# The gated recurrence of a fused kernel, its steps written in another order: transposes between the score halves, counts last, three score banks

## The chip, the cores and the metric

The kernel runs on one core of one Trainium2 chip. The time is the device time of one execution in microseconds, the median of several runs. The profile is of one further execution, and its times are microseconds from the start of its span. PE is the tensor engine, DVE the vector engine, ACT the scalar engine, POOL the GpSimd engine and SP the engine that issues most of the loads.

## The reference

Two blocks follow one another. The first is a gated linear recurrence over the sequence, for each of 4 batches and 8 heads with 768 positions and 48 channels. The second sends each of the 3072 rows to one of 8 experts.

```python
f = 1.0 / (1.0 + np.exp(-f_logit))                       # (4, 8, 768, 48)
for t in range(S):
    state = f[:, :, t, :, None] * state + np.einsum('bhd,bhe->bhde', k[:, :, t], v[:, :, t])
    y[:, :, t] = np.einsum('bhd,bhde->bhe', q[:, :, t], state)

x = y.transpose(0, 2, 1, 3).reshape(3072, 384)
logits = x @ w_gate                                       # (3072, 8)
expert_idx = np.argmax(logits, axis=1)
gate_w = softmax(logits)[np.arange(N), expert_idx]        # with 1e-9 in the denominator
for e in range(8):                                        # rows sorted by expert
    y_sorted[lo:hi] = np.maximum(x_sorted[lo:hi] @ w1[e], 0.0) @ w2[e]   # 384 -> 1024 -> 384
out = gate_w[:, None] * y_sorted[inv_perm]
```

## The kernel before

**The units.** The sequence is cut into 6 chunks of 128 positions, and the batches into two pairs, which gives 12 units (`NU = 12`). A unit holds two batches with 8 heads each; two heads lie above one another on the 128 partitions, so that a tile has 8 segments (`SEG`) of 128 positions, 1024 columns. Each unit has tiles `q`, `k`, `v` and `f`, all float32, of half a megabyte each. Units u and u + 2 follow one another in the sequence: the state of one is the input of the other.

**What is done to a unit.** The functions, with their lines:

- `growth` (L361, L362): ACT takes exp(-f), and POOL adds one, which gives 1/f.
- `product` (L369): a DVE scan multiplies these up along the positions into the tile `r`. There is one `r` for all units, so the scan of a unit waits until everybody has read the `r` of the unit before.
- `by_r` (L381, L382): POOL multiplies `k` by `r`, and copies the last column.
- `log_r` (L386) and `decay` (L392, L395): ACT takes the logarithm of `r` and the exponential of its negative, with a load of its function table before each; POOL copies the last column.
- `by_decay` (L400): DVE multiplies `q` by it.
- `score` (L412, L415): PE multiplies k and q into score tiles `s`, and DVE copies them with the causal mask into `at`. Here a score tile takes two banks of the accumulator, and there are two such tiles (the pool `pss`).
- `keys` (L427, L428): PE transposes `k` into two tiles `kp`, and ACT copies them into `kn`.
- `within` (L436) and `before` (L457): PE sums the output `yt` from the scores and v, and from the old state and q.
- `added` (L473) and `update` (L488, L490, L491): PE multiplies `kn` and v into `dp`, DVE adds the old state, and POOL multiplies the sum by the last decay.
- `settle` (L498): ACT copies `yt` into `ys`.
- `rows` (L518, L528, L533, L535): PE turns `ys` into rows with gate logits (`xp`), ACT copies the rows into `xr`, and DVE sums the logits into `lg`.

The small tiles `kp`, `xp`, `dp`, `rp` and `etp` share the pool `pst` under one tag, with two banks before.

**The routing.** For every second unit (and for each of the last two) `rows` returns a `Route` with methods that are called through the step: `choose` (DVE, L189 to L197) finds the expert of each row, `count` (PE, L201, L202) sums the chosen ones into `rp`, `place` (DVE, L208 to L226) turns the sums into positions, `weigh` (ACT, L229) and `fill` (DVE, L233 to L235) give the weights, and `send` (POOL, L164) scatters the rows into a buffer in memory.

**The order.** The loop over `n` runs 14 steps, from 0 to 13. Step n takes the scores of unit n, the outputs of unit n - 1 and the rows of unit n - 2, and it prepares units n + 1 and n + 2. The whole stretch stands under `manual_schedule` with all five engines: each engine runs its instructions in the order in which the code is written, and the planner adds only the waits. So a step's order is that of the calls in the loop, for each engine by itself.

Before the loop the first unit is prepared in halves (`ab`). The constants come in by four kinds of loads on ACT's queue: a mask (`mpack`), a table of 537.5 KB (`fpack`) with the identity and much else, and four pieces of the gate's weights that are written into `fpack`. These loads are written outside the written order, so the planner places them.

**The experts.** From step 12 on the first two expert tiles run between the last steps (`widen`, `narrow`; L266 and L280), and then 22 tiles of 128 rows, each with 48 matmuls of L266 and 16 of L280. The change does not touch these.

Of the kernel before, what the change touches and what calls it, by code (L numbers as in the profile page):

```python
# [19 lines left out]
C = 128  # L20
# [92 lines left out]
def kernel(  # L113
# [21 lines left out]
    nc.scalar.dma_start(mpack, nc.inline_tensor(mv, name="c_mpack").ap())  # L135
    nc.scalar.dma_start(fpack, nc.inline_tensor(fv, name="c_fpack").ap())
# [15 lines left out]
    halves = [(a, slice(DP * a, DP * a + D)) for a in range(2)]  # L152

    for a, r in halves:
        for b, cols in enumerate((slice(XW, WX), slice(0, E))):
            nc.scalar.dma_start(
                wx[r, :, cols],
                moe_w_gate.rearrange("(p two d) e -> two d p e", two=2, d=D)[a ^ b],
            )
# [167 lines left out]
    with ExitStack() as st:  # L327
        ld = st.enter_context(tc.tile_pool(name="ld", bufs=4))
        wk = st.enter_context(tc.tile_pool(name="wk", bufs=2))
        pss = st.enter_context(tc.tile_pool(name="pss", bufs=2, space=PSUM))  # L330
        psy = st.enter_context(tc.tile_pool(name="psy", bufs=1, space=PSUM))
        pst = st.enter_context(tc.tile_pool(name="pst", bufs=2, space=PSUM))
# [72 lines left out]
        def score(u):  # L405
            x = units[u]
            x["at"] = scores[u % 2]
            for a in range(2):
                ps = pss.tile([128, 2, HP, C], F32, name="s")
                for p, h, r in heads():  # L410
                    s = HP * a + p
                    nc.tensor.matmul(  # L412
                        ps[:, h, p], lhsT=x["k"][r, s], rhs=x["q"][r, s], start=True, stop=True
                    )
                nc.vector.copy_predicated(  # L415
                    x["at"][:, a].rearrange("p h s c -> p (h s) c"),
                    _bc(causal, 1, SEG),
                    ps.rearrange("p h s c -> p (h s) c"),
                )

        def keys(u):
            x = units[u]
            x["kn"] = wk.tile([128, SEG, C], F32, name="kn", bufs=1)
            for a in range(2):
                kp = pst.tile([128, HP, C], F32, name="kp", **tr)
                for p in range(HP):
                    nc.tensor.transpose(kp[:, p], x["k"][:, HP * a + p], ident)  # L427
                nc.scalar.copy(x["kn"][:, HP * a : HP * a + HP], kp)  # L428
# [120 lines left out]
        load(2, "fkqv")  # L549
        for part in ab:  # L550
            growth(0, part)
        for part in ab:
# [4 lines left out]
        for t in scores:  # L557
            nc.vector.memset(t, 0.0)
# [4 lines left out]
        product(1)  # L563

# [440 lines left out]
```

## Time and profile before

| what | value |
|---|---|
| median of 3 runs | 457.75 us (456.74 to 458.6) |
| the profiled execution | 455.68 us |
| its span in the profile | 453.8 us |
| PE busy | 409.9 us (90%) |
| DVE, ACT, POOL busy | 160.6, 124.0, 115.6 us |
| granted clock of PE, mean | 0.963 |
| first score matmul (unit 0) | 16.3 us |
| first score matmul of unit 11 | 136.5 us |
| first expert matmul of L280 | 161.2 us |

The page of a profile gives busy times by engine, the same in 40 slices, the chain of work that ended last, and groups of instructions by line. The trace behind it answers further questions: the timeline shows each instruction with its start, its length and, in square brackets, the idle time of its engine before it with the one that ended it; a view by stretches gives the busy time of each engine between chosen moments, with the granted clock of PE (1.00 is full speed). PEld is the loading of weights into PE, which overlaps its matmuls. A float32 matmul is two instructions in the trace, a transpose one.

### The profile page before, as it was taken

The numbers are of one execution on the slowest core, as the hardware profiler recorded it, in microseconds if no ns is written. First come the engines' busy times: TensorE is split into PE (matmuls) and PEld (weight loads), VectorE is DVE, ScalarE is ACT, GpSimd is POOL, SyncE is SP. The second block draws the span as 40 slices with busy tenths as digits, with TensorE's granted clock in tenths as the row PEclk, the third lists the DMA queues.
The fourth block names the chain that finished last, engine by engine and source line by source line (L and its number), as shares of the span: only waits on it lengthen the run. The fifth ranks groups of instructions, "written<-read, shape, count | busy, mean of one in ns | idle before, by whom it ended". The sixth has DMA issues, their size and how long they took to land.

```text
span 453.8 us, 8502 instructions
## 1 busy us (share of the span) xinstructions
PE 409.9 (90%) x3580; PEld 330.1 (73%) x3581; DVE 160.6 (35%) x325; ACT 124.0 (27%) x184; POOL 115.6 (25%) x133
## 2 busy tenths in 40 slices
PE   0478898989898998999999999999999999999992
PEld 0478787878797885888888888847688887777460
DVE  3866969494964452111111111122111122111110
ACT  3689787676764300000000000001000000000010
POOL 3654466666653420001100000000100000000000
PEclk9969998888979998999999999999999999999998
DMA  8999985597922233989991550730189999000000
GB/s 288 402 381 390 378 311 187 216 382 310 361 78 85 81 113 94 402 318 358 387 361 39 189 181 19 236 114 1 42 300 396 393 390 374 28 17 19 17 2 21
DMA packets 42861, 98.32 MB, mean 217 GB/s; under 512 B 3856, under 2 KB 27717, under 8 KB 42816
## 3 DMA queue, kind: packets, MB, share of 16 engines
q1 hardware_dynamic: 38496, 87.48, 52.9%
q0 software_dynamic: 3200, 9.64, 5.6%
q10 hardware_dynamic: 1120, 0.59, 0.4%
q8 instruction: 29, 0.48, 0.4%
q14 instruction: 16, 0.13, 0.1%
HBM read 81.46 MB, written 16.63 MB: 216 GB/s over the span
## 4 chain that ended last, share of the span: by engine, by line
PE 81%; ACT 10%; DVE 3%; issue 2%; POOL 1%; DMA 1%; POOLq 0%; ACTq 0%
PE hps L266 26%; PE yps L280 25%; PE s L412 6%; PE xp L518 5%; PE dp L473 3%; ACT L392 3%; PE yp L280 3%; ACT f L392 2%; PE s L266 2%; PE hps L785 2%; PE yps L813 2%; ACT f L361 2%; PE etp L253 2%; PE yt L457 2%; ACT xr L528 1%
## 5 line engine op out<-in xcount | busy, mean ns | idle before, releaser
L266 PEld LDWEIGHTS hps<-xT,w1t 128*128 128x128 f32 x1056 | 121.1, 192 | 7.3 <-issue 2.3
L266 PE MATMUL hps<-xT,w1t 128*128 128x128 f32 x1056 | 121.8, 275 | 0.0
L280 PE MATMUL yps<-w2t,hT 128*128 128x384 f32 x352 | 117.2, 486 | 0.0
L280 PEld LDWEIGHTS yps<-w2t,hT 128*128 128x128 f32 x352 | 65.2, 190 | 40.8
L164 POOL DMA_INDIRECT out_dram<-ysb,dst x26 | 25.3, 971 | 257.3 <-DVE ysb L287 257.3
L274 ACT ACTIVATE hT<-hps 128x512 f32<-128x512 f32 x22 | 13.1, 597 | 222.6 <-PE hps L266 222.6
L276 DVE TENSOR_SCALAR hT<-hps 128x512 f32<-128x512 f32 x22 | 15.2, 692 | 106.2 <-PE hps L266 101.1
L412 PE MATMUL s<-q,k 64*128 64x128 f32 x384 | 33.2, 340 | 16.7 <-POOL last L395 16.3
L287 DVE TENSOR_SCALAR ysb<-yps,xrow 128x384 f32<-128x384 f32 x22 | 13.6, 618 | 92.9 <-PE yps L280 92.9
L412 PEld LDWEIGHTS s<-q,k 64*128 64x128 f32 x384 | 30.6, 246 | 17.3 <-POOL last L395 16.0
L369 DVE TENSOR_TENSOR_SCAN r<-f,cap 128x1032 f32<-128x1032 f32 (+1 forms) x13 | 28.7, 2208 | 13.6 <-POOL f L362 13.6
L415 DVE COPY_PREDICATED at<-mpack,s 128x1024 f32<-128x1024 uint8 x24 | 30.6, 1312 | 6.1 <-PE s L412 6.1
L164 POOL DMA_INDIRECT xs<-xr,posi x24 | 26.4, 1098 | 21.6 <-DVE xr L235 6.8
L381 POOL TENSOR_TENSOR k<-k,r 128x1024 f32<-128x1024 f32 (+1 forms) x13 | 26.4, 2030 | 2.5 <-DVE r L369 2.4
L518 PE MATMUL xp<-fpack,ys 128*128 128x104 f32 x192 | 24.3, 280 | 0.8 <-ACT ys L498 0.8
L518 PEld LDWEIGHTS xp<-fpack,ys 128*128 128x128 f32 x192 | 22.4, 192 | 2.4 <-ACT ys L498 1.0
L436 PE MATMUL yt<-at,v 128*64 128x128 f32 x384 | 23.7, 277 | 0.0
L436 PEld LDWEIGHTS yt<-at,v 128*64 128x64 f32 x384 | 20.8, 138 | 1.3 <-issue 0.2
L473 PE MATMUL dp<-v,kn 128*64 128x48 f32 x320 | 14.7, 259 | 6.8 <-ACT kn L428 6.8
L473 PEld LDWEIGHTS dp<-v,kn 128*64 128x64 f32 x320 | 13.3, 172 | 9.6 <-ACT kn L428 8.3
L400 DVE TENSOR_TENSOR q<-q,f 128x1024 f32<-128x1024 f32 (+1 forms) x13 | 14.7, 1136 | 14.0 <-ACT f L392 14.0
L427 PE MATMUL kp<-fpack,k 128*128 128x128 f32 x96 | 14.4, 285 | 4.7 <-ACT kn L428 2.8
(108 smaller groups left out, 361.3 us busy)
## 6 DMA issues: line engine op xcount, KB each, us to landing
qw<-in_moe_w_dram SPq DMA_DIRECT2D x16, 1536.0 KB, 12.3
w1t<-in_moe_w_dram SPq DMA_DIRECT2D x8, 1536.0 KB, 8.8
w2t<-in_moe_w_dram SPq DMA_DIRECT2D x8, 1536.0 KB, 13.1
xs<-pad SPq DMA_DIRECT2D x8, 800.0 KB, 12.9
v<-in_vu_dram SPq DMA_DIRECT2D x12, 512.0 KB, 6.4
f<-in_fu_dram SPq DMA_DIRECT2D x11, 516.0 KB, 8.2
k<-in_ku_dram SPq DMA_DIRECT2D x11, 512.0 KB, 9.0
q<-in_qu_dram SPq DMA_DIRECT2D x11, 512.0 KB, 6.5
```

Source lines behind the costliest of these rows:

```text
L164: ins = nc.gpsimd.indirect_dma_start(out=dst, out_offset=bass.IndirectOffsetOnAxis(ap=idx, axis=0), in_=src, in_offset=None, bounds_check= ...
L266: nc.tensor.matmul(hp[g][:, f, :], lhsT=w[0][:, j, b * 128 : b * 128 + 128], rhs=x["xT"][:, j, :], start=j == 0, stop=j == KD - 1,)
L276: nc.vector.tensor_scalar(x["hT"][:, 4:8], hp[1], 0.0, None, op0=OP.max)
L280: nc.tensor.matmul(yp, lhsT=x["hT"][:, f, :], rhs=w[1][:, f, :], start=f == 0, stop=f == NF - 1)
L369: nc.vector.tensor_tensor_scan(x["r"][:, part].rearrange("p s c -> p (s c)"), x["f"][:, part].rearrange("p s c -> p (s c)"), cap[:, part]. ...
L381: nc.gpsimd.tensor_tensor(k, k, r[:, :, 1:CR], op=OP.mult)
L392: nc.scalar.activation(dec, dec, AF.Exp, scale=-1.0)
L412: nc.tensor.matmul(ps[:, h, p], lhsT=x["k"][r, s], rhs=x["q"][r, s], start=True, stop=True)
L415: nc.vector.copy_predicated(x["at"][:, a].rearrange("p h s c -> p (h s) c"), _bc(causal, 1, SEG), ps.rearrange("p h s c -> p (h s) c"),)
L436: nc.tensor.matmul(x["yt"][DP * (h ^ a) : DP * (h ^ a) + DP, a, p], lhsT=x["v"][:, a, 2 * p + h], rhs=x["at"][:, a, h, p], start=p == 0, s ...
L473: nc.tensor.matmul(x["dp"][r, s], lhsT=x["kn"][:, s, r], rhs=x["v"][:, a, 2 * p + h, 0:D], start=s == 0, stop=True, skip_group_check=True,)
L518: nc.tensor.matmul(xp[:, p], lhsT=x["ys"][:, a, p], rhs=wx[:, p, 0:XW] if a else wx[:, p, E:WX], start=True, stop=True,)
```

## The change

The steps of the loop get another order, with some pools and loads:

- The scores of a unit are taken in two halves, and the transposes `keys` with their copies (now a function of its own, `keep`) stand between them. Each half has two tiles of one bank, and DVE copies each by itself. The pool of score tiles has three banks, the pool `pst` three.
- `product` of unit n + 2 moves from late in the step to behind the scores; `decay` comes before `within`; `before` follows `within` directly.
- `by_decay` is done in halves, and comes after `before`, ahead of `added` and `update`.
- `count`, `place` and `fill` come last in a step, after `update`.
- `growth` runs for unit n + 3 in place of n + 2, and f is loaded one unit further ahead, apart from k, q and v.
- Ahead of the loop the two `scores` tiles are zeroed before the first exponential, one on DVE and one on POOL, and the constants are loaded after the two halves of the first `growth`, in the written order.

The core of the diff:

```diff
-    nc.scalar.dma_start(mpack, ...)
-    nc.scalar.dma_start(fpack, ...)
...
+    def load_consts():
+        nc.scalar.dma_start(mpack, nc.inline_tensor(mv, name="c_mpack").ap())
+        nc.scalar.dma_start(fpack, nc.inline_tensor(fv, name="c_fpack").ap())
+        for a, r in halves:
+            for b, cols in enumerate((slice(XW, WX), slice(0, E))):
+                nc.scalar.dma_start(wx[r, :, cols], moe_w_gate...[a ^ b])
...
-        pss = st.enter_context(tc.tile_pool(name="pss", bufs=2, space=PSUM))
+        pss = st.enter_context(tc.tile_pool(name="pss", bufs=3, space=PSUM))
-        pst = st.enter_context(tc.tile_pool(name="pst", bufs=2, space=PSUM))
+        pst = st.enter_context(tc.tile_pool(name="pst", bufs=3, space=PSUM))
...
-        def score(u):
+        def score(u, a):
...
+            ps = [pss.tile([128, HP, C], F32, name="s") for h in range(2)]
+            for p, h, r in heads():
+                s = HP * a + p
+                nc.tensor.matmul(
+                    ps[h][:, p], lhsT=x["k"][r, s], rhs=x["q"][r, s], start=True, stop=True
                 )
+            for h in range(2):
+                nc.vector.copy_predicated(x["at"][:, a, h], _bc(causal, 1, HP), ps[h])
...
+        def keep(u):
+            for a in range(2):
+                nc.scalar.copy(units[u]["kn"][:, HP * a : HP * a + HP], units[u]["kp"][a])
...
         load(2, "fkqv")
+        load(3, "f")
+        nc.gpsimd.memset(scores[1], 0.0)
+        nc.vector.memset(scores[0], 0.0)
         for part in ab:
             growth(0, part)
+        load_consts()
...
-        for t in scores:
-            nc.vector.memset(t, 0.0)
...
         growth(1)
         product(1)
+        growth(2)
```

The loop's step before and after, without the expert pieces of steps 12 and 13 (the sends of a count are queued after `fill` in both):

```python
# before
score(n); settle(n-2); by_r(n+1); log_r(n+1); one send
rows(n-2); choose; within(n-1); count
decay(n+1); growth(n+2); weigh; by_decay(n+1)
keys(n); place; fill; product(n+2)
before(n-1); added(n); update(n); load(n+3, "fkqv")

# after
settle(n-2); score(n, 0); by_r(n+1); log_r(n+1); one send
keys(n); keep(n); score(n, 1); product(n+2)
rows(n-2); choose; decay(n+1); growth(n+3); weigh
within(n-1); before(n-1); by_decay(n+1) in halves
added(n); update(n); count; place; fill
load(n+4, "f"); load(n+3, "kqv")
```

## The prediction

> **What bounds the kernel now.** I read the page first, for the shares and for section 2, then busy time by stretch, with the stretches cut at the first score matmul (L412) of each step, then the chain of work, then the timeline of VectorE (DVE) and GpSimd (POOL).
>
> The stretches. Columns: stretch, length, busy time of PE, PEld, DVE, ACT and POOL with instruction counts, granted clock, DMA share, GB/s.
>
> ```profile
> 35.00:56.40 21.40, 17.82 (x286) 16.04 (x282) 16.86 (x30) 17.91 (x26) 10.87 (x12) 1.00 1.02 386
> 78.60:102.60 24.00, 21.95 (x312) 19.71 (x310) 17.31 (x30) 17.52 (x26) 14.81 (x16) 0.86 0.82 304
> 102.60:126.50 23.90, 21.84 (x310) 19.63 (x310) 17.11 (x33) 17.42 (x26) 14.80 (x16) 0.86 0.87 327
> 72.09:75.50 3.41, 2.08 (x25) 1.70 (x29) 2.92 (x9) 2.66 (x5) 3.10 (x4) 0.98 0.19 73
> 75.50:78.91 3.41, 3.41 (x61) 2.96 (x54) 3.31 (x6) 2.32 (x4) 0.72 (x1) 0.50 0.50 159
> ```
>
> The steps start at 16.3, 27.0, 35.2, 44.7, 56.4, 65.9, 78.6, 89.8, 102.6, 113.8, 126.5 and 136.5 us (n = 0 to 11); the first expert matmul of L280 starts at 161.2. A pair of steps took 21 us early and 24 us later. The difference is the clock: it stands at 0.50 for 6.7 us in each late pair (75.4 to 82.2, 99.3 to 106.1, 123.2 to 130.0), and each time it fell after 3.4 us in which PE was busy 2.1. From 180 us to the last tiles PE is hardly ever without work, and nothing there is changed, so the change moves only the moment at which the experts begin.
>
> The chain through one pair. Columns: start, length, work.
>
> ```profile
> 63.35 0.95 ACT f L361
> 64.31 0.48 ACT kn L428
> 64.83 1.16 PE dp L473 x32
> 65.99 1.99 PE s L412 x32
> 67.98 1.99 PE xp L518 x16
> 69.98 0.54 ACT xr L528 x2
> 70.55 1.28 ACT L392
> 71.84 1.06 ACT f L392
> ...
> 75.15 1.65 PE yt L457 x32
> 76.80 1.88 PE dp L473 x32
> ```
>
> A step is a ring over PE and ACT: `dp` waits for the copies `kn`, these stand on ACT behind two exponentials, these behind `xr`, which waits for `xp`, and `xp` for the scores. Its sum is 9.5 us, against 9.0 us of PE work at full clock (s 1.98, xp 1.98, yt 1.9, kp 1.03, the part on the old state 1.02, dp 1.07); a count adds 0.43. The last two lines run at half clock.
>
> The timeline of DVE and POOL. Columns: start, length, engine, line, operation.
>
> ```profile
> 9.08 1.18 POOL L381 TENSOR_TENSOR k<-k,r 128x512 f32<-128x512 f32 x1
> 9.15 2.20 DVE L369 TENSOR_TENSOR_SCAN r<-f,cap 128x516 f32<-128x516 f32 x1 [2.96 <-POOL f L362]
> 10.20 1.13 POOL L382 COPY rend<-r 128x4 f32<-128x4 f32 x1
> ...
> 74.92 1.35 DVE L223 TENSOR_TENSOR place<-place,oh 128x32 f32<-128x32 f32 x1
> 74.99 0.22 POOL L395 COPY last<-f 128x8 f32<-128x8 f32 x1
> 75.15 1.07 POOL L362 TENSOR_SCALAR f<-f 128x1032 f32<-128x1032 f32 x1
> ...
> 47.33 0.83 POOL L491 TENSOR_TENSOR state<-state,last 128x384 f32<-128x384 f32 x1 [2.88 <-DVE state L490]
> 48.11 2.19 POOL L381 TENSOR_TENSOR k<-k,r 128x1024 f32<-128x1024 f32 x1
> ```
>
> A DVE instruction with two SBUF operands stands still while POOL works. The scan of 516 takes 1.23 us in its first form, 2.20 here, and it ends one scan after POOL's `k`; `rend`, 0.19 us elsewhere, waits for the scan in turn. L223 takes 0.19 us where POOL is idle, 1.35 here, ending as POOL ends. So DVE and POOL exclude each other, and what POOL runs beside the small DVE work of a count has a price.
>
> **The change part by part.** *Constants.* ACT now issues them after both growth exponentials, in a written order. The four gate loads write into `fpack` and so wait for it (4.6 us to land), then take 4 x 0.46 us of ACT's queue; behind them stand `log_r`, `decay` and so the first score. Second Exp done by 5.5 to 6.0, `fpack` issued 0.4 later, landed at 10.5 to 11.0, gates out at 12.3 to 12.9, then table 1.28, two Ln 1.2, table 1.28, Exp 0.63, multiply 0.62: first score at 17.4 to 17.9, against 16.3. Freed on the other side: the two memsets of 1.76 us that held DVE from 11.7 to 15.6; one stays on DVE and one goes to POOL, both ahead of the first load's landing at 3.6 (uncovered they would cost up to 3.5).
>
> *Steps 0 to 3.* Step 0 goes from the last Exp (17.6): growth 1.05, POOL 1.05, scan 2.31, `by_r` 2.38, scan 2.3, half a multiply 0.63, some gaps: step 1 starts at 27.7, before 27.0. Then PE work of 6, 8 and 9.4 us, with DVE close behind, ends step 3 near 54.4, before 56.4: **-2.0 us**. f for unit 6 is now the bound load. 0.5 MB more stand ahead of it than of f for unit 5, which landed at 52.07: 1.3 us at 390 GB/s, so 53.4, and ACT wants it at about 53. I take nothing; at worst 1.5.
>
> *The ring.* Transposes now come between the score halves, so `kn` is copied long before `dp`: the 9.5 us ring is gone. The kp, kn, dp and s instructions stay as many; DVE's two 1.31 us copies become four of about 0.66, its multiply two of 0.63. No wait is gained for ACT, whose own work per step (two tables 2.56, three functions 3.17, copies 3.1) is 8.9 us.
>
> *Counts last.* This adds the wait. DVE does the update (0.53) and only then the eight placing instructions; the update releases POOL's state multiply (0.83), and `by_r` of the next step (2.18) stands right behind it, its scan long done. In the trace that multiply starts 0.09 us after the update and `by_r` 0.05 us before it ends. Place and fill take 1.7 us by the late step where POOL is idle (143.23 to 144.89). From the update's end U: POOL is taken until U + 3.3; L210 waits for the multiply at least, L223 for `by_r`; L223 and the four after it take another 0.9. Lower end U + 2.0 (no exclusion), upper U + 5.1 (DVE loses every gap and the +1 of L362 is in front too). I take U + 4.3, by the nearest rows, where L223 lost both gaps between three POOL instructions, at 75, 99 and 123 us.
>
> Behind the placing on DVE stand the next step's score copies, and behind these, with three banks, PE: the second half of the scores needs a fourth bank, so the first copy's end. A step after a count then runs: U + 4.3, copy 0.66, half scores 1.05, `xp` 1.98, `xr` 0.6, table 1.28, Exp 1.06, multiply 1.25, update 0.53 = **12.7 us** to the next update. The other step runs POOL 3.3, scan 2.3, `lg` 0.4, choose 1.3 (141.35 to 142.54), multiply 1.25, update 0.53 = 9.1, or 10.1 if the +1 gets between the halves of the multiply; I take **9.6**.
>
> *The clock.* In the long step PE finishes the transposes at about U + 1.1 and gets its next matmul at U + 5.0: 3.9 us idle, where 1.35 us in a window brought the clock down. A slow stretch cost (1.65 - 1.02) + (1.88 - 1.07) + (3.69 - 1.98) = 3.15 us of PE work; here it falls on scores, `xp` and `yt`, all on the path: 3.0 (ends 0 and 3.3).
>
> Steps 4 to 10 hold four long and three short ones: 4 x 15.7 + 3 x 9.6 = 91.6 us, against 136.5 - 56.4 = 80.1: **+11.5**.
>
> *Tail.* From step 11 no POOL multiply follows an update. PE's work to L280 is 8.5 + 2.0 + 1.9 + 0.8 + 1.0 + 0.4 + 2.2 + 2.0 + 2.8 + 0.4 + 0.8, with 0.3 of waits 23.1 us, against 24.7: **-1.6**. The load split adds no bytes; each issue is 0.33 to 0.45 us on SP, which is ahead of its users.
>
> Sum: -2.0 + 11.5 - 1.6 = +7.9. The profiled execution took 455.68 (span 453.8, 1.9 around it); the median is 457.75. Added to the median: 465.7, so 466.
>
> The Trainium skill (SBUF — State Buffer, section "Who interferes with whom") says that a VectorE instruction with two SBUF inputs and a GpSimd one that reads SBUF exclude each other, and whoever issues first keeps the shared ports for the whole instruction; by it the placing waits whenever POOL was first. The page does not say who wins a gap between two POOL instructions. The skill (TensorE: Matmul & The Clock Gate, section "HAM oscillation") warns of PE gaps over some 3.4 us; the rows above show the clock falling after two gaps of 0.6 and 0.8 us close together. By the page alone the kernel before would show no slow stretch, and the new one would.
>
> **The rivals.**
> 1. *The placing is not held up* (DVE finds POOL free or wins). For: L190, with two SBUF operands, took only 0.24 us beside `k` at 50.11. Against: L223. The long step becomes 10.8, PE-bound, the short 9.4, the clock stays up: 4 x 10.8 + 3 x 9.4 = 71.4, -8.7; with the other terms -12: 446. It decides from a placing that ends under U + 2.3. Chance 0.14.
> 2. *DVE wins both gaps* because the +1 delays POOL: place at U + 2.5, PE gap 2.3 us, clock still falls: 4 x (11.3 + 2.1) + 3 x 9.45 = 82, -1.7 in all: 456. For: the scan at 9.15 got in ahead of `rend`. Chance 0.16.
> 3. *Held up, but the clock stays at 1.0*: 4 x 12.7 + 3 x 9.6 = 79.6, so -4: 454. For: PE was busy only 1.91 of 3.41 us at 51.61 and the clock held. Chance 0.10.
>
> **How the numbers follow.** Forecast 466, chance 0.60; its own range 459 to 474 (upper end: place at U + 5.1, short steps 10.1, stretch 3.3, start 1.5 later). Rival 1 ends the range at 446. Below and above it I leave 0.15. A measurement of this kernel can tell about 0.5%, 2.3 us. Faster: rival 1, most of 3, a third of 2 and a little doubt in the forecast, 0.28; same 0.10; slower 0.62.
>
> **What would show it.** Right: L223 or L210 of 2 us and more in steps 3, 5, 7, 9, inside POOL's `state` and `k`; in the step after, a wait of PE's second score half for a DVE `at` of 3 to 5 us; PEclk 0.5 after it; pairs of 25 us; `kn` no longer before `dp` in the chain. Wrong: L223 under 0.7 us there, PEclk 1.0 from 50 us on, pairs near 20 us. The first score should start at 17 to 18 us.

## The result and the profile after

| what | before | after |
|---|---|---|
| median of 4 runs each | 457.26 us | 462.29 us (461.70 to 462.58) |
| profiled execution, its span | 455.68, 453.8 us | 462.27, 460.4 us |
| mean granted clock of that execution | 0.963 | 0.973 |
| first score matmul (unit 0) | 16.3 us | 20.8 us |
| steps 0 to 3 | 40.1 us | 40.1 us |
| steps 4 to 10 | 80.1 us | 86.2 us |
| first score of unit 11 to the first expert matmul (L280, now L282) | 24.7 us | 22.9 us |

The change made the kernel 1% slower: the ratio is 1.0104, with a 95% interval of 1.0078 to 1.013. A kernel's runs spread with their mean granted clock (the kernel before: 449.4 us at 0.986, 460.1 at 0.959), so the ratios, here and below, compare only the runs within 1.5% of the fastest of their kernel, and differ from the quotients of the medians by up to 0.9%. The forecast was 466, with a range of 446 to 474. The two profiled executions differ by 6.6 us: +4.5 at the start, +6.1 in steps 4 to 10, -1.8 in the tail, -2.5 in the first expert tiles, where the kernel before had a wait of 0.7 us and a slow stretch at 174 to 178 us and the changed one has neither, and +0.3 later. Lines of the changed kernel are a few higher: the scores are L413 and L417, `place` L210 to L228, `fill` L235 to L237, the update L493 and L494, `by_r` L383.

The stretches of the changed kernel: two pairs of steps, then windows of 3.41 us. Columns: stretch, length, busy time of PE, PEld, DVE, ACT and POOL with instruction counts, granted clock, DMA share, GB/s.

```profile
60.87:85.90 25.03, 22.55 (x309) 20.40 (x309) 18.67 (x36) 17.37 (x27) 15.50 (x17) 0.86 0.58 204
110.85:132.68 21.83, 19.35 (x310) 17.28 (x309) 18.50 (x36) 17.14 (x27) 14.46 (x16) 1.00 0.96 348
63.59:67.00 3.41, 1.06 (x14) 0.96 (x14) 2.88 (x8) 1.10 (x3) 2.22 (x3) 1.00 0.84 312
67.00:70.41 3.41, 3.41 (x17) 3.39 (x16) 3.41 (x4) 0.48 (x1) 1.26 (x3) 0.50 0.32 126
111.37:114.79 3.42, 2.08 (x22) 1.60 (x19) 3.28 (x7) 3.29 (x4) 3.25 (x4) 1.00 1.06 405
114.79:118.20 3.41, 2.27 (x24) 2.15 (x25) 2.92 (x8) 0.01 (x1) 2.31 (x4) 1.00 1.04 414
```

One pair takes 25.0 us and another 21.8 with the same instructions. PE's work is 19.35 us at full clock, so that even the fast pair holds 2.5 us of waiting. In the slow pair a window with 1.06 us of PE work is followed by the clock at 0.50. In the fast pair the same wait is cut in two by a window's edge at 114.79 us: 2.08 and 2.27 us of work, and the clock stays.

The chain of work, first at the start and then through a count. Columns: start, length, work.

```profile
4.58 9.01 DMA fpack<-c_fpack
...
13.62 0.37 ACTq L157
...
15.51 1.28 ACT L388
...
61.13 0.47 DVE counts L210
61.60 0.09 DVE counts L211
...
61.71 0.76 DVE sums L212
...
62.74 1.81 DVE place L225
...
65.28 0.62 DVE at L417
...
65.94 1.16 PE s L413 x14
67.09 3.67 PE xp L521 x16
70.77 3.40 PE yt L439 x32
```

At the start ACT waits nine microseconds for `fpack`, and the logarithm's table comes only at 15.51. In the step the chain no longer holds `kn` and `dp`: it runs from DVE's update through the placing into the score copy and then into PE, whose `xp` takes 3.67 us at half clock.

The timeline of DVE, POOL and PE at the same place. Columns: start, length, engine, line, operation, and in brackets the idle time before it.

```profile
60.58 0.55 DVE L493 TENSOR_TENSOR state<-dp,state 128x384 f32<-128x384 f32 x1
61.05 0.55 DVE L210 COPY counts<-fpack 128x8 f32<-128x8 f32 x1
...
61.71 0.75 DVE L212 TENSOR_TENSOR_SCAN sums<-fpack,counts 128x40 f32<-128x40 f32 x1
...
62.74 1.80 DVE L225 TENSOR_TENSOR place<-place,oh 128x32 f32<-128x32 f32 x1
64.58 0.19 DVE L228 TENSOR_REDUCE posi<-place 128x4 int32<-128x32 f32 x1
...
65.10 0.18 DVE L237 RECIPROCAL xr<-su 128x4 f32<-128x4 f32 x1
...
60.37 1.20 POOL L364 TENSOR_SCALAR f<-f 128x1032 f32<-128x1032 f32 x1 [0.27 <-ACT f L363]
61.54 0.82 POOL L494 TENSOR_TENSOR state<-state,last 128x384 f32<-128x384 f32 x1
62.33 2.17 POOL L383 TENSOR_TENSOR k<-k,r 128x1024 f32<-128x1024 f32 x1
...
65.94 1.16 PE L413 MATMUL s<-q,k 64*128 64x128 f32 x14 [2.48 <-DVE at L417]
```

L225 stands still until POOL's `k` is done, as the forecast had it for L223. Two instructions ahead of it waited as well, L210 until the end of POOL's addition (L364) and L212 until the end of its multiply of the state. The placing ends at 65.28, which is 4.15 us after the update's end at 61.13, and PE has waited 2.48 us for the score copy behind it.

### The profile page after: what moved, and what is told of

It reads as the page before. It is cut to its first block, busy times and chain, and to the rows that moved or that the text cites. A ratio compares the mean times of both kernels' runs of the same rounds, so it can differ in the third digit from the quotient of the medians.

```text
span 460.4 us, 8555 instructions
## 1 busy us (share of the span) xinstructions
PE 412.5 (90%) x3580; PEld 333.1 (72%) x3581; DVE 168.0 (36%) x359; ACT 123.3 (27%) x184; POOL 118.2 (26%) x134
## 4 chain that ended last, share of the span: by engine, by line
PE 78%; DVE 10%; issue 3%; ACT 3%; DMA 3%; POOL 0%; ACTq 0%; POOLq 0%; DVEq 0%
PE hps L268 26%; PE yps L282 25%; PE s L413 5%; PE xp L521 4%; PE yt L439 3%; PE s L268 2%; PE hps L796 2%; PE yps L824 2%; PE yp L282 2%; DMA fpack<-c_fpack 2%; DVE at L417 2%; PE etp L255 2%; DVE place L225 2%; PE kp L426 2%; DVE r L371 2%
## 5 line engine op out<-in xcount | busy, mean ns | idle before, releaser
L282 PE MATMUL yps<-w2t,hT 128*128 128x384 f32 x352 | 117.2, 486 | 0.0
L282 PEld LDWEIGHTS yps<-w2t,hT 128*128 128x128 f32 x352 | 65.2, 190 | 40.8
L413 PE MATMUL s<-q,k 64*128 64x128 f32 x384 | 34.8, 312 | 36.4 <-POOL last L397 21.7
L413 PEld LDWEIGHTS s<-q,k 64*128 64x128 f32 x384 | 28.7, 210 | 40.2 <-POOL last L397 25.4
L278 DVE TENSOR_SCALAR hT<-hps 128x512 f32<-128x512 f32 x22 | 15.2, 691 | 105.9 <-PE hps L268 105.9
L289 DVE TENSOR_SCALAR ysb<-yps,xrow 128x384 f32<-128x384 f32 x22 | 13.6, 618 | 93.3 <-PE yps L282 93.3
L417 DVE COPY_PREDICATED at<-mpack,s 128x512 f32<-128x512 uint8 x48 | 32.2, 724 | 12.5 <-PE s L413 12.5
L166 POOL DMA_INDIRECT xs<-xr,posi x24 | 27.5, 1147 | 22.9 <-DVE lg L538 8.9
L521 PE MATMUL xp<-fpack,ys 128*128 128x104 f32 x192 | 29.4, 317 | 0.2 <-ACT ys L501 0.2
L521 PEld LDWEIGHTS xp<-fpack,ys 128*128 128x128 f32 x192 | 27.2, 226 | 1.7 <-issue 0.4
L383 POOL TENSOR_TENSOR k<-k,r 128x1024 f32<-128x1024 f32 (+1 forms) x13 | 27.1, 2086 | 3.4 <-DVE r L371 3.4
L439 PE MATMUL yt<-at,v 128*64 128x128 f32 x384 | 26.8, 299 | 0.0
L439 PEld LDWEIGHTS yt<-at,v 128*64 128x64 f32 x384 | 23.9, 153 | 1.5 <-issue 0.6
L402 DVE TENSOR_TENSOR q<-q,f 128x512 f32<-128x512 f32 x24 | 17.2, 757 | 21.2 <-ACT f L394 21.2
L397 POOL COPY last<-f 128x8 f32<-128x8 f32 (+1 forms) x13 | 9.9, 768 | 46.1 <-ACT f L394 46.1
L364 POOL TENSOR_SCALAR f<-f 128x1032 f32<-128x1032 f32 (+1 forms) x13 | 14.7, 1136 | 3.3 <-ACT f L363 3.3
## 6 DMA issues: line engine op xcount, KB each, us to landing
w2t<-in_moe_w_dram SPq DMA_DIRECT2D x8, 1536.0 KB, 13.6
```

Source lines behind the costliest of these rows:

```text
L166: ins = nc.gpsimd.indirect_dma_start(out=dst, out_offset=bass.IndirectOffsetOnAxis(ap=idx, axis=0), in_=src, in_offset=None, bounds_check= ...
L278: nc.vector.tensor_scalar(x["hT"][:, 4:8], hp[1], 0.0, None, op0=OP.max)
L282: nc.tensor.matmul(yp, lhsT=x["hT"][:, f, :], rhs=w[1][:, f, :], start=f == 0, stop=f == NF - 1)
L383: nc.gpsimd.tensor_tensor(k, k, r[:, :, 1:CR], op=OP.mult)
L402: nc.vector.tensor_tensor(q, q, x["dec"][:, part], op=OP.mult)
L413: nc.tensor.matmul(ps[h][:, p], lhsT=x["k"][r, s], rhs=x["q"][r, s], start=True, stop=True)
```

## The experiments

Theory: the placing, now behind the update, is shut out by POOL's two multiplies; with three score banks PE's second half of the scores waits for it; and that wait brings the clock down. Besides, the start is late because the constants stand in ACT's order. The rivals are in the expectations. PSUM is the accumulator whose banks the pools `pss` and `pst` share out; the other tiles lie in SBUF. Medians are over all runs. The columns on the right are the lengths of steps in the profiles, in us.

| kernel | median us | ratio to before, 95% | steps 4, 6, 8, 10 | step 5 |
|---|---|---|---|---|
| before | 457.26 | 1 | 9.5, 11.2, 11.2, 10.1 | 12.7 |
| changed | 462.29 | 1.0104 [1.0078, 1.013] | 15.3, 15.2, 12.1, 14.4 | 9.7 |
| changed, again (e5) | 461.01 | 1.0116 [1.0049, 1.0182] | 13.7, 13.7, 12.1, 14.4 | 9.7 |
| e1 two tiles in PSUM | 455.72 | 1.0034 [0.9981, 1.0087] | 13.2, 11.6, 13.2, 11.6 | 9.7 |
| e2 constants early | 454.75 | not given | 14.1, 13.7, 12.1, 14.6 | 9.7 |
| e3 counts ahead of the update | 448.33 | 0.9886 [0.9852, 0.9921] | 10.3, 10.4, 10.4, 9.7 | 10.5 |
| e4 four score banks | 450.53 | 0.9957 [0.992, 0.9995] | 10.3, 14.0, 10.3, 9.6 | 9.7 |
| e6 three tiles in PSUM | 448.31 | 0.9817 [0.9764, 0.987] | 10.0, 10.0, 10.0, 11.3 | 9.7 |
| e7 wait filled with PE work | 453.63 | 0.9961 [0.9925, 0.9997] | 12.1, 12.1, 12.1, 12.1 | 9.7 |
| e8 is e3 with e2 | 440.96 | 0.9654 [0.9603, 0.9706] | 10.2, 10.4, 10.4, 9.9 | 10.5 |
| e9 is e8, transposes back | 453.53 | 0.9984 [0.9938, 1.003] | 10.6, 10.6, 10.6, 9.0 | 12.1 |
| e10 is e8, exponentials back | 472.76 | 1.0384 [1.0321, 1.0448] | 11.3, 14.2, 15.5, 15.5 | 13.9 |
| e11 before, three tiles in PSUM | 459.57 | 1.0046 [0.9997, 1.0095] | 11.0, 11.0, 11.0, 9.8 | 12.9 |
| e12 is e6 with e2 | 439.32 | 0.9651 [0.9605, 0.9698] | 10.0, 10.0, 10.0, 9.8 | 9.7 |

The medians of the kernel before beside these were 456.68 (e1 to e4), 456.43 (e5 to e8) and 456.76 us (e9 to e12). e1 to e4 ran on another chip than e5 to e12, so where they are compared with the repeated run (e5), the comparison rests on these medians being alike.

### e1: two tiles of the placing in PSUM

```diff
-            counts = self.pool.tile([128, E, n + 1], F32, name="counts")
+            counts = self.pc      # a piece of the bank of rp
...
-            at = self.t("place", E)
+            at = self.pa          # another piece
```

> The changed kernel, with the tiles counts and place moved from SBUF into the PSUM bank that already holds rp, so that the scan of the counts and the multiply by oh read one operand from SBUF and one from PSUM. Nothing else is different. Theory (the placing stands still because its instructions with two SBUF operands are shut out while POOL multiplies the state and k, and PE's second half of the scores stands behind it): the scan of the counts falls from 0.75 to about 0.25 us and the multiply from 1.80 to about 0.2, the placing ends about 2 us after the update instead of 4.15, PE's wait before the second half of the scores falls from 2.5 us to under 1, the long steps fall from 15.3 to about 11, no stretch at clock 0.50 is left between 60 and 150 us, and the time is 447 to 450 us. Rival 1 (the three banks for the scores are the cause, not the placing): the placing gets shorter and the time stays at 462. Rival 2 (the wait itself goes but the clock would have been what it is anyway): the long steps fall by 2 us only, 454 us.

The scan and the multiply became short (0.75 to 0.24 us, 1.80 to 0.20), but the time fell by 5.3 us against the repeated run of the changed kernel, where 12 and more were expected. The timeline of DVE and POOL in this kernel:

```profile
61.28 0.24 DVE L217 TENSOR_TENSOR_SCAN sums<-fpack,rp 128x40 f32<-128x40 f32 x1
...
61.81 0.20 DVE L230 TENSOR_TENSOR rp<-rp,oh 128x32 f32<-128x32 f32 x1
...
62.15 0.18 DVE L240 TENSOR_REDUCE su<-ex 128x4 f32<-128x32 f32 x1
62.36 1.97 DVE L241 TENSOR_SCALAR su<-su 128x4 f32<-128x4 f32 x1
...
62.14 2.17 POOL L388 TENSOR_TENSOR k<-k,r 128x1024 f32<-128x1024 f32 x1
```

The multiply, now 0.20 us, got through, and the addition of a constant to four numbers per partition took its place and waited out POOL's `k`. It has one tensor operand. The theory of two operands was too narrow: an addition with its one source and its target in SBUF is shut out too, while the sum of L240, also from SBUF to SBUF, ran beside `k` in 0.18 us. PE still waited 1.93 us, and the clock fell twice. The first rival fails, as the time did move; the second is left open here, since the wait did not go.

The Trainium skill (SBUF — State Buffer, section "Who interferes with whom") says that copies and additions of a constant can take the shared ports too, and that the sums along a row never do. L241 and L240 agree with it; the prediction had drawn on the same section for two operands alone.

### e6: su as well

```diff
-            su = self.t("su")
+            su = self.ps          # a third piece of the bank
```

> As the first experiment (counts and place in the PSUM bank of rp), with su moved there as well, so that no instruction of the placing and the filling has only SBUF operands except the first small copy of the base. In the first experiment the scan and the multiply were short (0.24 and 0.20 us), but the next instruction with only SBUF operands, the addition to su on 128 x 4 elements, took 1.97 us and ended as POOL's k and rend ended, so the chain ended at the update's end plus 3.6 us instead of 4.15. Theory (any such instruction is shut out while POOL works, and the exclusion accounts for about 2 us of the 4.15): the addition takes 0.2 us, the chain ends at 1.7 to 2.0 us after the update, PE's wait before the second half of the scores falls to 0.2 to 0.6 us, the long steps to 10 to 10.5 us, the clock stays up, and the time is 448 to 451 us. Rival (the place in the order behind the update costs, whatever POOL does): PE's wait stays over 1.5 us and the time over 454.

The timeline of DVE and PE in e6:

```profile
63.06 0.20 DVE L232 TENSOR_TENSOR rp<-rp,oh 128x32 f32<-128x32 f32 x1
...
63.82 0.17 DVE L243 TENSOR_SCALAR rp<-rp 128x4 f32<-128x4 f32 x1
...
64.88 1.16 PE L420 MATMUL s<-q,k 64*128 64x128 f32 x14 [0.35 <-DVE at L424]
```

This is the test of the mechanism. The order is that of the change, POOL's instructions are the same, and only where three small tiles lie is different. The chain ends 2.0 us after the update (62.2 to 64.2, against 4.15), PE's wait falls from 2.48 to 0.35 us, the steps from 12.1 (where the clock held) to 10.0, and no slow stretch is left between 46 and 440 us. The time is 12.7 us less than that of the changed kernel in the same runs. The rival, that the order costs whatever POOL does, asked for a wait over 1.5 us. In step 10 alone the wait stayed (11.3 us): there the last count is followed by a comparison of 1 x 2 elements, both operands in SBUF, which took 1.19 us behind `k`.

### e3: the counts ahead of the update again

The edit, condensed:

```diff
+            if rt: rt.count(...)              # ahead of by_decay
             by_decay(n + 1) in halves
+            if rt: rt.place(); rt.fill()
             if here < NU and here // 2 < NC - 1:
                 added(here)
                 update(here)
-            if rt: rt.count(...); rt.place(); rt.fill()
```

> The changed kernel, with the count's matmuls ahead of by_decay and the placing directly behind by_decay, ahead of the update, as the order was before the change; the transposes between the score halves, the three banks and the exponentials further ahead stay. Theory (what costs is that the placing stands behind the update, whose POOL multiply and by_r shut it out): the placing takes 1.7 to 2 us because POOL has nothing to do there but the +1, the update comes 1.5 to 2 us later in that step, the wait of PE's second score half for DVE falls under 1 us, the pairs of steps take about 22 us instead of 25, and the time is 452 to 455 us. Rival 1 (the three banks are the cause): the wait of PE's second score half stays at 2 to 3 us and the time at 461 or more. Rival 3 (the +1 of 1.2 us on POOL shuts the placing out in this place too, as it did to the multiply of 1.35 us in the kernel before): pairs of 23 to 24 us with a stretch of clock 0.50, about 458 us.

The timeline of DVE and PE in e3:

```profile
60.24 1.03 DVE L210 COPY counts<-fpack 128x8 f32<-128x8 f32 x1
...
61.90 0.19 DVE L225 TENSOR_TENSOR place<-place,oh 128x32 f32<-128x32 f32 x1
...
62.74 0.53 DVE L493 TENSOR_TENSOR state<-dp,state 128x384 f32<-128x384 f32 x1
...
63.96 1.16 PE L413 MATMUL s<-q,k 64*128 64x128 f32 x14 [0.65 <-DVE at L417]
```

The one edit is worth 12.7 us against the repeated run, and the time lies under the range expected. The placing takes 2.6 us, 1.0 of it a copy of 128 x 8 elements that waits for POOL's +1; then the update follows, and PE waits 0.65 us. The pairs are 20.5 to 20.8 us, shorter than the 22 expected, as the update, which now starts 2.0 us after the next step's first score instead of 0.3 us before it, holds PE up by those 0.65 us only. The +1 shuts out one small copy, not the multiply, so the third rival's 458 us did not come.

### e4: four banks for the scores

```diff
-        pss = st.enter_context(tc.tile_pool(name="pss", bufs=3, space=PSUM))
+        pss = st.enter_context(tc.tile_pool(name="pss", bufs=4, space=PSUM))
-        pst = st.enter_context(tc.tile_pool(name="pst", bufs=3, space=PSUM))
+        pst = st.enter_context(tc.tile_pool(name="pst", bufs=2, space=PSUM))
```

> The changed kernel, with four banks for the scores and two for the other small products (three and three after the change). Theory (the placing holds DVE, PE only meets it at the first copy of a score): PE issues the second half of the scores at once, so its wait moves behind it, to the value matmuls that need the masked scores and to the products that now share two banks; half of the 2.5 us is filled with score matmuls, the clock stays up in one or two of the gaps, and the time is 453 to 460 us with the placing's multiply still at 1.8 us. Rival 1 (three banks are the whole cause): the wait is gone, the pairs of steps take 20 to 21 us, and the time is 447 to 450 us. Rival (two banks for xp, kp, dp and counts are too few): new waits of PE for ACT's copies of 1 us and more in each step, 465 us and more.

The timeline of DVE and PE in e4, from steps 4 and 6:

```profile
61.96 1.82 DVE L225 TENSOR_TENSOR place<-place,oh 128x32 f32<-128x32 f32 x1
...
80.68 3.42 DVE L210 COPY counts<-sums 128x8 f32<-128x8 f32 x1
...
84.86 0.63 PE L426 MATMUL kp<-fpack,k 128*128 128x128 f32 x4 [3.02 <-DVE place L222]
```

The placing is held up as before (1.82 us), and PE hardly notices (0.24 us): with a fourth bank the second half of the scores goes out at once. This came nearer to the rival's number than to the theory's. Both are right in part: the loss needs DVE late and PE out of banks, and either cure is worth 10 to 13 us against the 461.0 of the repeated run. Where the copy of the base lost both gaps, 3.42 us behind the state and `k`, the two remaining small banks ran out instead, PE waited 3.02 us for that of `rp`, and the clock fell (step 6, 14.0 us).

### e2: the constants at their old place

```diff
+    load_consts()
     nc.gpsimd.memset(pad, 0.0)
...
             growth(0, part)
-        load_consts()
```

> The changed kernel, with the constants and the gate loads issued at their old place, outside the written order of ACT, so that ACT issues them ahead of the first growth. Nothing else is different. Theory (the first score came 4.5 us later than before because fpack took 9.0 us to land and the gate loads, the table and log_r stand behind it on ACT): the first score comes at 15.5 to 17 us instead of 20.8 and the time is 457 to 459 us, 4 us less than after the change. Rival (the start is late because of the halved first loads or the moved memsets): the first score stays at 20 to 21 and the time at 462.

The first score came at 15.1 us instead of 20.8, somewhat before the range expected. The median was 6.3 us below that of the repeated run (461.01), more than the 4 expected, but its four runs go from 449.0 to 459.8, so the price rests on the start in the profile. `fpack` took 4.8 us to land here and 9.0 in the changed kernel. So the constants account for the whole of the late start, and the moved memsets cost nothing (the first loads are halved in the kernel before as well): without the constants' wait the changed start is 1.3 us earlier than that of the kernel before.

### e5 and e7: what the clock costs

e5 is the changed kernel once more; e7 repeats its transposes into the wait:

```diff
-                for p in range(HP):
-                    nc.tensor.transpose(kp[:, p], x["k"][:, HP * a + p], ident)
+                for again in range(3 if u in (4, 6, 8, 10) else 1):
+                    for p in range(HP):
+                        nc.tensor.transpose(kp[:, p], x["k"][:, HP * a + p], ident)
```

> The changed kernel once more, unchanged, beside the runs of the kernels that undo a part. Theory (how much time is lost depends on how often the clock falls in a run, and that differs from run to run: the runs of the kernel before went from 449.4 to 460.1 us as their mean granted clock went from 0.986 to 0.959): the median is 456 to 462 us, the spread of the runs several us, and the step starts in the profile differ from the first profile only where the clock fell. Rival (each kernel has its own fixed stretches of slow clock): 462 us again, within 0.5 us, with the stretches at the same places (66, 90 and 138 us).

> The changed kernel, with the eight transposes of k issued three times over in steps 4, 6, 8 and 10, into the same bank with the same result: 2.2 us of extra PE work that falls into the wait of 2.5 us before the second half of the scores and nowhere else. Theory (the gap is what brings the clock down, and the low clock costs 2 to 3 us in a long step): the clock stays at 1.00 from 60 to 150 us, all long steps take 12.1 to 12.4 us instead of 15.3, 15.2, 12.1 and 14.4, and the time is 8 us less than that of the changed kernel in the same runs where those show three stretches. Rival (the clock falls for a reason other than the idle PE, or its fall costs nothing because the wait alone sets the step): the long steps stay at 14 to 15 us and the time does not move, or rises by 1 us.

In e5 the wait was 2.47 to 2.62 us in all four long steps again. The clock fell for 3.4 us where it had fallen for 6.8 in two of them, at 66.5 and 90.4 us, again not in step 8, and once more in step 10. So the rival is half right: the places are those of the waits, but the lengths differ, and the times went from 458.3 to 464.5 us. A long and a short step in the stretch view of e7:

```profile
61.37:83.22 21.85, 21.10 (x325) 19.02 (x325) 18.52 (x36) 17.36 (x27) 15.11 (x17) 1.00 0.66 234
```

PE does 16 more transposes in the long step, which change no result, its wait there falls to 0.75 us, the clock stays at 1.00 in all four long steps, each takes 12.13 us, and the kernel is 7.4 us faster than e5. The rival of e7 falls, and with it the second one of e1: the clock costs 1.6 to 3.2 us in a step in which it falls, on top of the wait, and it falls because PE is idle.

### e8, e9 and e10: what the rest of the change is worth

> The changed kernel with two parts undone: the count and the placing stand ahead of the update again (third experiment), and the constants are issued outside ACT's written order (second experiment). The transposes between the score halves, the three banks and the exponentials further ahead stay. Theory (these two parts cost what the change lost, and the rest of it gains): first score at 15 us, pairs of steps of 20.5 us, no stretch of slow clock after 60 us, first narrow matmul of the experts at about 150 us, and a time of 442 to 445 us, faster than the kernel before by 2.5% or more. Rival (an earlier start runs into the loads, which end at the bandwidth of the chip): 446 to 449 us, as the third experiment alone, with PE waiting for a loaded q, k or f in steps 3 to 6.

e8 gave 440.96 us, a little under the range, and 20 us under the changed kernel: the gains of e3 (12.7) and e2 (6.3) nearly add up to that. On this base the other two parts of the change were undone, one at a time (the edits, condensed):

```diff
# e9
-                keys(here); keep(here)        # between the score halves
...
             by_decay(n + 1) in halves
+            if here < NU: keys(here); keep(here)
# e10
-        growth(2)                             # ahead of the loop
-            if n + 2 < NU: product(n + 2)     # behind the scores
-            if n + 3 < NU: growth(n + 3)
+            if n + 2 < NU: growth(n + 2)
             place; fill
+            if n + 2 < NU: product(n + 2)
             added(here); update(here)
```

> The eighth kernel (counts ahead of the update, constants early), with one more part undone: the transposes of k and their copies stand again behind both halves of the scores, behind by_decay, as before the change. Theory (the transposes between the halves are what the change gains by, since the copies kn no longer stand on ACT between two exponentials and the matmul dp): dp waits for kn again by 1 to 2 us in each step, pairs of steps take 22.5 to 24 us instead of 20.6, the clock falls again in some pairs, and the time is 449 to 456 us, against 441 for the eighth kernel. Rival (the gain comes from the exponentials further ahead alone): pairs of 20.5 to 21 us and 441 to 443 us.

In e9 a pair takes 22.7 us, and the time is 12.6 us over that of e8. The clock fell once in its profile, at 36.6 us, and not in the pairs from 60 us on. The timeline of PE, ACT and DVE in e9, from a short and a long step:

```profile
69.38 1.16 PE L477 MATMUL dp<-v,kn 128*64 128x48 f32 x32 [0.48 <-ACT kn L432]
...
81.47 1.14 PE L477 MATMUL dp<-v,kn 128*64 128x48 f32 x32 [1.52 <-ACT ys L502]
...
79.54 1.07 ACT L432 COPY kn<-kp 128x512 f32<-128x512 f32 x2
...
81.16 0.21 DVE L223 TENSOR_TENSOR place<-rp,sums 128x32 f32<-128x32 f32 x1
```

In the short step `dp` waits 0.48 us for the copies `kn`, less than the 1 to 2 expected. In the long step it waits 1.52 us, but `kn` is done at 80.61. `dp` starts 0.86 us later, and 0.10 us after the placing's L223, which is the last to read `rp`; steps 3 and 7 show the same. With the transposes behind the count, `dp` is the third tile after `rp` in the pool of three banks and takes over its bank. So half of that wait is for a bank that the placing holds, not for ACT. Of the 12.0 us between the profiles of e9 and e8, 5.8 lie in steps 0 to 3, where the clock fell, 4.5 in steps 4 to 10 and 1.8 in the tail.

> The eighth kernel, with the growth (its exponential and POOL's +1) and the product scan two units ahead at the old place, the scan behind the placing and ahead of the update, instead of three units and two units ahead near the start of the step; the transposes stay between the halves. The loads are not changed. Theory (the scan of 2.3 us is put between the placing and the update and waits there for the +1, so the update and the first score copies of the next step come 1 to 2 us later): pairs of 22 to 23 us and 447 to 453 us. Rival (PE has 9.0 us of work in a step and the transposes alone are enough): pairs of 20.5 us and 441 us.

e10 came out 20 us above its range, the largest miss of these expectations. The direction and the mechanism hold, and the price was far too low. The timeline of DVE and PE in e10:

```profile
61.77 2.28 DVE L372 TENSOR_TENSOR_SCAN r<-f,cap 128x1032 f32<-128x1032 f32 x1
63.96 0.53 DVE L494 TENSOR_TENSOR state<-dp,state 128x384 f32<-128x384 f32 x1
...
65.19 1.16 PE L414 MATMUL s<-q,k 64*128 64x128 f32 x14 [1.68 <-DVE at L418]
```

The scan stands between the placing and the update, and the score copies behind both, so PE waits 1.7 to 3.4 us in every step from 4 on, not in every second, and the clock falls seven times. So on this base the transposes between the halves are worth 12.6 us (the wait for the bank included) and the exponentials and scans further ahead 31.8 us. They were not run alone on the kernel before, and these are prices in this order only: the kernel before has its scan between the placing and the update too, and took 16 us less than e10.

### e11 and e12: the same tiles in the kernel before, and the best order

> The kernel before the change, with only counts, place and su moved into the PSUM bank of rp. Theory (POOL's +1 shuts the placing out in the kernel before too, 0.7 to 1.35 us in steps 3, 5, 7 and 9, and the transposes of k stand behind it): the multiply of the placing takes 0.2 us, but the transposes then wait for kn on ACT, which ended only 0.2 us earlier, so that steps 5, 7 and 9 become 0 to 0.5 us shorter, the slow stretches of 6.8 us stay in most pairs, and the time is within 3 us of the kernel before, 453 to 457 in the same runs. Rival (the shutting out is what brings the clock down in the kernel before): no stretch of slow clock between 60 and 150 us, pairs of 21 us instead of 24, and 446 to 449 us.

The timeline of DVE and PE in e11:

```profile
77.69 0.20 DVE L230 TENSOR_TENSOR rp<-rp,oh 128x32 f32<-128x32 f32 x1
...
77.14 0.66 PE L434 MATMUL kp<-fpack,k 128*128 128x128 f32 x4 [1.00 <-ACT kn L435]
```

In the kernel before, the multiply of 1.35 us became 0.20, and nothing was gained: 459.57 against 456.76 us, within the 3 us but outside the 453 to 457 expected, with an interval that just holds no change. PE there waits for ACT's `kn`, 1.00 us, and the slow stretches of 6.8 us stayed. (The profile is of a run of 461.68 us; here the odd steps, which hold the count, are the long ones.) The price that POOL put on the placing was off the path before the change, and on it after.

> The order of the change is kept (counts last, behind the update), with the placing's tiles counts, place and su in PSUM (sixth experiment), the constants issued outside ACT's written order (second experiment), and the three small instructions on lack, some and fix moved from the last count to behind the next step's score copies, since the first of them took 1.19 us behind POOL's multiply of k in the sixth experiment. Theory (with the shutting out gone, the order of the change is better than the old order by the 0.7 us that PE waits for the placing in the eighth kernel): first score at 15 us, pairs of 19.7 us, all steps 9.7 to 10.0, no slow stretch after 60 us, and 438.5 to 440.5 us, 1 us less than the eighth kernel's 441. Rival (the loads bound the steps once they take 9.7 us): a wait for f, q or k in steps 4 to 7, and 441 to 443 us.

A pair of steps in the stretch view of e12, columns as above:

```profile
56.15:75.85 19.70, 19.35 (x309) 17.28 (x309) 16.23 (x36) 17.27 (x27) 16.92 (x17) 1.00 0.79 292
```

e12 keeps the change's order with the three tiles in PSUM, the constants early, and the comparison after the last count moved behind the next scores. A pair takes 19.70 us, of which PE works 19.35, so the rival's wait for the loads did not come. The median of 439.32 us is the lowest, 3.5% under the kernel before (interval 3.0 to 4.0%). Between e12 and e8 lie 1.6 us in the medians, with runs of 438.4 to 441.3 against 440.9 to 441.4, but their ratios to the kernel before are the same (0.9651 and 0.9654): which of the two orders is better is not shown.

## Why the forecast was right, and which terms were off

**The placing held up (the forecast's case).** It was put to end at U + 4.3 (U is the end of the update) and ended at U + 4.15. L225 took 1.80 us, just under the 2 us asked for, because the waiting was spread over L210 (0.55, behind the addition L364) and L212 (0.75, behind the state) as well: DVE got through in both gaps between POOL's three instructions, where the forecast went by rows in which it lost them, and the end came out the same because L225 ran into `k`. The short steps came at 9.72 for 9.6, the long ones without the clock's fall at 12.1 for 12.7, and `kn` left the chain. e6 shows the cause: without the shutting out the same order gives 10.0.

**PE's wait.** 3.9 us was forecast, 2.48 measured. The end was right (U + 5.0, measured U + 4.8); the beginning was not, as PE finished its first score half, the transposes and one more score matmul only at U + 2.3, having reached the scores late itself.

**The clock.** Four falls at 3.0 us were forecast. There were three, of 3.2, 3.1 and 2.3 us (15.3, 15.2 and 14.4 against 12.1). This is most of why steps 4 to 10 cost +6.1 instead of +11.5: four long and three short steps of the forecast make 91.6, the measured ones 86.2, and 3.4 of the difference are in the clock, 2.4 in the long steps' base; the short ones were 0.4 more than forecast. The forecast took a window's fall from the length of PE's wait alone; where the wait lies against the windows decides too.

**The start, a mis-sized term.** First score at 17.4 to 17.9 was forecast, 20.8 measured. The landing of `fpack` was priced at 4.6 us, from a row of the kernel before in which it was issued ahead of nearly everything; now it is issued at 4.58, in the middle of the loads of units 0 and 1, and took 9.0. The rest of that chain was right: 13.6 to 20.8 is 7.2 us, for the 6.9 forecast.

**Steps 0 to 3.** They were to take 36.8 us from the first score on, and took 40.1, as before. The forecast's sum does not reach its own end: 27.7 and PE work of 6, 8 and 9.4 us make 51.1, and the 3.3 us from there to 54.4 have no term of their own. PE waited 2.1, 1.6 and 1.0 us at the first scores of units 1, 2 and 3 for DVE and POOL, and the first score matmuls of unit 1 ran at half clock (2.08 us for 16, where 1.16 is the full-clock time). With the start this made s of unit 4 come 6.5 us later than forecast (60.9 for 54.4), and it balanced the clock.

**The tail** was -1.8 for -1.6. The forecast's statement that nothing changes from the experts on missed 2.5 us: the kernel before had a slow stretch at 174 to 178 us.

**The sum.** Of the forecast's terms, start and steps 0 to 3 were 6.5 us too low, steps 4 to 10 5.4 too high, and the experts 2.2 too high. The forecast of +7.9 against +6.6 in the profiles and +5.0 in the medians owes its closeness to terms that cancelled, which is luck; the mechanism of the long steps was the right one.

**The rivals' prices** could be tried. The third, a placing held up while the clock stays, was put at 454; e7, which makes that case, took 453.6. Here too terms cancelled: unit 4 began 7.0 us later than forecast (61.4 for 54.4), steps 4 to 10 took 77.7 for 79.6, the experts 2.2 less, and the kernel before beside it was 1.3 us faster than the 457.75 from which the sum started. The first, a placing not held up, was put at 446; e6 took 448.3. With its start at 17.6 in place of 20.5 it would, by estimate, have come about 3 us lower. What spoke for that rival was weak: L190, at 50.11, met only the last 0.19 us of `k` (48.11 to 50.30).

## What to carry to other kernels

A group of tiny instructions that is moved has to be priced by what the neighbour engine runs at its new place, operand by operand: each one whose data lie in SBUF alone may wait for a whole instruction of POOL (up to 1.97 us behind one, though the sums along a row never did here), and moving three small tiles to PSUM was worth as much as undoing the move. A wait of DVE cost PE 2.48 us where it had no bank left to run ahead and 0.24 where it had one, so the bank count and the order are one decision. A load that moves from the start into the middle of other loads must be given a landing time from there, not its own old one (9.0 us here for 4.6).

## What the hardware did that was not expected

**Which small instructions wait.** Beside POOL's multiplies these were held up: a scan and a multiply with two SBUF operands (0.75 and 1.80 us), a copy of 128 x 8 (3.42, from POOL's addition through both multiplies; 0.55 and 1.03 beside the addition alone) and an addition of a constant on 128 x 4 (1.97). These were not: sums from SBUF to SBUF (0.18, L240 of e1), and the small ones with PSUM on one side (0.16 to 0.24 in e6). Who wins the gap between POOL's state and `k` was not fixed: in the changed kernel L212 got through at the end of the state, and L225, which came later, was caught by `k`; in e4 the copy of the base lost both. What decides it stays open.

**The clock goes by fixed windows.** Every slow stretch in these profiles away from the end of the span lasted 3.41, 6.83 or 10.24 us, and within one profile they start on one grid of 3.41 us (67.0, 90.9 and 138.7 in the changed kernel, 7 and 14 windows apart). Between 57 and 150 us, over all profiles, the clock fell after every one of the 19 windows with less than 1.87 us of PE work, after none with 2.0 or more, and after five of the eight between. The row of the prediction from 72.09, with 2.08 us, starts 0.11 us behind the edge of its window; the clock fell at 75.39, and the window before that holds 1.97 us in the stretch view of the kernel before:

```profile
71.98:75.39 3.41, 1.97 (x24) 1.59 (x28) 2.89 (x10) 2.66 (x5) 3.04 (x4) 1.00 0.21 79
```

A wait of 2.48 us thus brought the clock down or not, by where the edge lay: 1.06 us of work in the window at 63.59, 2.08 and 2.27 in the two at 111.37.

The Trainium skill (TensorE: Matmul & The Clock Gate, section "HAM oscillation") warns of PE gaps over some 3.4 us. Here gaps of 1.9 to 2.6 us sufficed, in the kernel before two of 0.8 us in a row (ahead of 75.39), and these measurements decide: it is the work in a window that counts, not the length of one gap.
